# Chunk 2's second norm in a product buffer, and its turn one step later, in a one-core attention and GLU block

## The chip, the cores and the metric

The program runs on one core of a Trainium2 chip. The metric is the device time of one execution in microseconds (us); lower is better. Three timed runs of the kernel before have a median of 546.23 us (546.02 to 546.67). The profile is that of one execution, which has a time of its own.

A core has five engines that run side by side, each through its own list of instructions in order: TensorE (PE) multiplies matrices and turns tiles, VectorE (DVE) and ScalarE (ACT) work on elements, GpSimd (POOL) and SyncE (SP) mostly issue transfers (DMA). An instruction that waits holds up everything behind it in its engine's list. PE writes its results to PSUM, eight banks that other engines must empty ("evict") before they can be used again.

## The reference

```
x: 2048 rows of 576, bf16
mod = silu(c) @ w_mod                      -> sa, ca, ga, sb, cb, gb
h = layernorm(x) * (1 + ca) + sa           first norm
q, k, v = h @ wqkv                         32 heads of 18
attention of each row to 8 rows: itself and 2, 4, ... 14 rows back
x = x + ga * (attention @ wo)              called x1 in the kernel
h = layernorm(x) * (1 + cb) + sb           second norm
x = x + gb * (((h @ w_gate) * (h @ w_up)) @ w_down)     width 4608
```

`layernorm(v) = (v - mean) / sqrt(var + 1e-5)` over the 576 columns of a row.

## The kernel before

**Chunks and stages.** The rows are cut into 8 chunks of 256, each of 2 tiles of 128 rows. The GLU runs in five stages over groups of tiles: stage 0 takes chunk 0 (tiles 0 and 1), stage 1 chunks 1 and 2 (tiles 2 to 5), and so on. Each stage is a `gate_up` (36 blocks of 128 of the GLU's columns, `hh = gate * up`) and then a `down_pairs` (the sums with `w_down`; the last stage uses `down_last`). What the later chunks need (norms, queries, keys, values, attention, the product with `wo`) is laid between the matmuls of these stages as "pieces".

**The order is written by hand.** Nothing reorders it: each engine runs its instructions in the order in which the Python code issues them. In `down_pairs` the work of stage 0 is a list of 32 steps (8 blocks of `w_down`, 4 steps each; line 988), and the table `dbg` (line 1507) says which pieces are issued behind which step: an entry `(24, norm_x1_2)` is issued behind step 24, and an entry with a list such as `(27, b_parts(1))` puts its first half behind step 27 and its second behind step 28. Behind the 32 steps come the last sums of the stage over the last four blocks: with two tiles (line 1007) these are the narrow sums `run("r", 0, 1)`, the wide ones `run("a", 0, 1)`, then both with the row halves changed over, `gate_r()` and `gate(0)`, `gate(1)` on DVE, and the stores.

**Row halves.** Every matmul uses 64 of the 128 rows of the PE array, and two run side by side, so a step issues pairs: a wide one (`acc`, 512 columns) and a narrow one (`accr`, 64 columns).

**Turning a chunk.** A norm `xn` has rows on partitions and the GLU needs columns on partitions. `turn_unit` (line 611) does this on PE: `first()` takes two PSUM banks and turns 12 squares of 64 x 128, `second()` turns 8 more and then evicts six pieces with the modulation, three on DVE (line 332) and three on ACT (line 334). `b_parts(2)`, kept as `t2_2` (line 1506), is this for chunk 2's second norm; it writes `h2T`, which the first matmul of stage 1's `gate_up` reads. In `dbg` its first half stands behind step 30 and its second behind step 31. Other chunks are turned by DMA: `a_flip(4)`, behind step 29, issues two transposing DMAs from SP that read chunk 4's first norm and write `hT`. `a_mod(4)` then modulates `hT` in place early in stage 1, three parts on DVE and two on ACT, for the units of chunk 4's queries and keys, which begin behind block 3 of that `gate_up`.

**Chunk 2's second norm.** `norm_x1_2` (line 1486), behind step 24: ACT takes tile 0's mean and variance (lines 316 to 323), writing what it doesn't need into `junk`, a buffer of the pool `prodp`; DVE takes tile 1's (lines 1497, 1498) and ACT the square root (lines 1499, 1500); then DVE writes both normalized tiles into `xn` (line 1503), a buffer of the pool `lnp`.

**Pools.** A tile of a pool takes over the buffer of an older tile, and its first write waits until the last use of the older one has ended. `lnp` has 2 buffers. When `norm_x1_2` asks for one, chunk 1's second norm (read by `b_parts(1)`, steps 27 and 28) and chunk 4's first norm (read by `a_flip(4)`, step 29) are both still in use. `prodp` has 6, for the attention's products of queries and keys (line 481), which no chunk makes during the end of stage 0. The next products are those of chunk 3, early in stage 1.

Of the kernel before, what the change touches and what calls it, by code (L numbers as in the profile page):

```python
# [18 lines left out]
P = 128  # L19
# [30 lines left out]
def kernel(  # L50
# [253 lines left out]
        nc.scalar.activation(rstd, rstd, ACTF.Ln, bias=eps[:], scale=1.0 / D)  # L304
        nc.scalar.activation(rstd, rstd, ACTF.Exp, scale=-0.5)

    act_mv = []

    def act_norm(src, junk=None):
        xn = lnp.tile([P, ST, DP], BF, name="ln_xn") if junk is None else None  # L310
        junk = xn if junk is None else junk
        mv = small.tile([P, ST, 2], F32, name="ln_mva")
        act_mv.append(mv)

        def mean(j):
            nc.scalar.activation(junk[:, j, 0:D], src(j), ACTF.Identity, scale=-1.0 / D, accum_out=mv[:, j, 0:1])

        def square(j):
            nc.scalar.activation(junk[:, j, 0:D], src(j), ACTF.Square, bias=mv[:, j, 0:1], accum_out=mv[:, j, 1:2])

        def rsq(r=slice(0, ST)):
            nc.scalar.activation(mv[:, r, 1], mv[:, r, 1], ACTF.Ln, bias=eps[:], scale=1.0 / D)
            nc.scalar.activation(mv[:, r, 1], mv[:, r, 1], ACTF.Exp, scale=-0.5)

        def norm(j):
            for d0, s0, n in ((0, 0, D), (D, D - 64, 64)):
                nc.vector.tensor_scalar(xn[:, j, d0:d0 + n], src(j)[:, s0:s0 + n], mv[:, j, 0:1], mv[:, j, 1:2], ALU.add, ALU.mult)
        return xn, mean, square, rsq, norm
# [360 lines left out]
    def b_parts(i, cols=(0, 1)):  # L689
        def make():  # L690
            ht, o0 = h2_of(ST * i + cols[0])
            return turn_unit(bb[i]["xn"], cols, mod_evict(lambda m: ht[:, m, o0:o0 + P * len(cols)], cols, 2))
        return parts(make)
# [12 lines left out]
    def a_flip(i):  # L706
        return lambda: (a_tiles(i), flips(aa[i]["hT"], aa[i]["xn"]))
# [236 lines left out]
    def down_pairs(gi, hh, bg):  # L944
        for piece in bg.get(-1, ()):
            piece()
        t0, t1 = GROUPS[gi]
        nj = t1 - t0
        steps = down_steps(nj)
        acc = [ps([P, 512], F32, "acc") for _ in range(2)]  # L950
        accr = [ps([P, 2, 64], F32, "accr") for _ in range(3 if nj == 3 else 2)]
        acc += [ps([P, 512], F32, "acc") for _ in range(nj - 2)]
        o_ts, t_r = {}, {}
        seen, written, order, synced = set(), {}, [0], [-1]
        left = {("a", j): 2 * FT for j in range(nj)} | {("r", j): 2 * FT for j in range(nj)}

        def mm(kind, j, r, f):
            bank = (kind, j) if kind == "a" else (kind, j % len(accr))
            dst = acc[j][:] if kind == "a" else accr[j % len(accr)][:, j // len(accr), :]
            cs = slice(0, 512) if kind == "a" else slice(512, D)  # L960
            last_r, n, m = written.get(bank, (r, -1, None))
            if last_r != r and n > synced[0]:
                swap_after(m)
                synced[0] = n
            rows = (LO, HI)[r]
            left[kind, j] -= 1
            m = half(dst, hh[rows, f, js(j)], wd_blk[gi * NBLK + f // FB][rows, f % FB, cs], bank not in seen, left[kind, j] == 0)
            seen.add(bank)
            written[bank] = (r, order[0], m)
            order[0] += 1  # L970

        def pair(kind, lo, hi):
            for r, (j, f) in enumerate((lo, hi)):
                mm(kind, j, r, f)

        def gate(j):
            o_ts[j] = gup.tile([P, 512], BF, name="o_t", tag="g_sb" if j % 2 else "u_sb")
            nc.vector.tensor_tensor(o_ts[j][:], acc[j][:], gb_bc[:, 0:512], ALU.mult)

        def gate_r():  # L980
            t = smp.tile([P, nj, 64], BF, name="t_r", tag="tree")
            for k, a in enumerate(accr):
                n = len(range(k, nj, len(accr)))
                nc.vector.tensor_tensor(t[:, k:nj:len(accr), :], a[:, 0:n, :],
                                        gb_bc[:, None, 512:D].to_broadcast([P, n, 64]), ALU.mult)
            t_r[0] = t

        for n, (lo, hi, r_early, loaded) in enumerate(steps):
            fs = list(zip(lo, hi))
            for k, (a, b) in enumerate(fs):  # L990
                if r_early and k == len(fs) - 1:
                    pair("r", a, b)
                    pair("a", a, b)
                else:
                    pair("a", a, b)
                    pair("r", a, b)
            if loaded is not None and (gi > 0 or loaded not in (4, 5)):
                load_wd((5, 6, NBLK - 1, 7)[loaded] if gi == 0 and loaded < 4 else gi * NBLK + loaded + 3)
            for piece in bg.get(n, ()):
                piece()  # L1000
        f0 = FT - FB

        def run(kind, a, b):
            for f in range(f0, FT):
                pair(kind, (a, f), (b, f))

        if nj == 2:
            run("r", 0, 1)
            run("a", 0, 1)
            run("r", 1, 0)  # L1010
            gate_r()
            run("a", 1, 0)
            gate(0)
            gate(1)
        elif nj == 4:
            run("r", 0, 1)
            run("r", 2, 3)
            run("a", 0, 1)
            run("a", 2, 3)
            run("r", 1, 0)  # L1020
            run("r", 3, 2)
            gate_r()
            run("a", 1, 0)
            gate(0)
            gate(1)
            run("a", 3, 2)
            gate(2)
            gate(3)
        else:
            for k, (lo, hi) in enumerate(cycle_of_three(f0)):  # L1030
                for a, b in zip(lo, hi):
                    pair("a", a, b)
                    pair("r", a, b)
                if k == 4:
                    gate(1)
            gate_r()
            gate(0)
            gate(2)
        assert not any(left.values())
        for j in range(nj):  # L1040
            xt = x1[(t0 + j) // ST][(t0 + j) % ST]
            r0 = (t0 + j) * P
            nc.vector.tensor_tensor(xt[:, 0:512], o_ts[j][:], xt[:, 0:512], ALU.add)
            nc.vector.tensor_tensor(xt[:, 512:D], t_r[0][:, j, :], xt[:, 512:D], ALU.add)
            nc.sync.dma_start(out_flat[r0:r0 + P, :], xt[:])
        load_wd(gi * NBLK + NBLK + 2)
# [404 lines left out]
    w1, w2, w3, w4, w5, w6, w7 = [w_parts(i) for i in range(1, NCH)]  # L1451
    n3, n1, n4, n2 = {}, {}, {}, {}

    def begin(n, src):
        n.update(zip(("xn", "mean", "square", "rsq", "norm"), act_norm(src)))

    def stat_act(n, tiles=range(ST)):
        for j in tiles:
            n["mean"](j)
            n["square"](j)  # L1460
# [23 lines left out]
        n4["rsq"]()  # L1484

    def norm_x1_2():
        src = lambda j: x1[2][j]
        junk = prodp.tile([P, ST, DP], BF, name="prod")
        _, mean, square, rsq, _ = act_norm(lambda j: src(j)[:], junk)
        xn = bb[2]["xn"] = lnp.tile([P, ST, DP], BF, name="ln_xn")  # L1490
        mva = act_mv[-1]
        stats, mv = small.tile([P, ST, 2, 6], F32, name="ln_statsb"), small.tile([P, ST, 2], F32, name="ln_mvb")
        mean(0)
        square(0)
        rsq(slice(0, 1))
        for hf in range(2):
            nc.vector.bn_stats(stats[:, 1, hf, :], src(1)[:, hf * 288:(hf + 1) * 288])
        nc.vector.bn_aggr(mv[:, 1, :], stats[:, 1].rearrange("p a b -> p (a b)"))
        nc.scalar.activation(mv[:, 0, 0:1], mv[:, 1, 1:2], ACTF.Ln, bias=eps[:])
        nc.scalar.activation(mv[:, 0, 1:2], mv[:, 0, 0:1], ACTF.Exp, scale=-0.5)  # L1500
        for j, m, r, op in ((0, mva[:, 0, 0:1], mva[:, 0, 1:2], ALU.add), (1, mv[:, 1, 0:1], mv[:, 0, 1:2], ALU.subtract)):
            for d0, s0, n in ((0, 0, D), (D, D - 64, 64)):
                nc.vector.tensor_scalar(xn[:, j, d0:d0 + n], src(j)[:, s0:s0 + n], m, r, op, ALU.mult)

    q3, k3, qk4_3, v0_3, v1_3 = qkv_units(3, [(0, 0, 5)])[0]
    t2_2 = b_parts(2)
    dbg = {0: at((-1, [gb_row]), (-1, lambda: n3["rsq"]()), (0, o_parts(1)), (0, lambda: (norms(n3), load_x(5))), (2, lambda: av(4)),
                 (5, a_parts(3)), (6, stat4), (6, lambda: av(2)), (8, w1[0]), (10, w1[1]), (11, stat1), (12, q3), (13, lambda: av(3)), (14, k3), (15, lambda: av(14)),
                 (16, qk4_3), (18, v0_3[:1]), (18, lambda: norms(n1)), (19, o_parts(2)), (20, lambda: (norms(n4), load_x(6))), (21, v0_3[1:]), (22, w2[0]), (23, w2[1]),
                 (24, norm_x1_2), (25, v1_3), (27, b_parts(1)), (29, a_flip(4)), (FT - FB - 2, t2_2)),  # L1510
           1: at((0, w3[0]), (3, w3[1]), (4, o_flip(4)), (4, lambda: b_ln(3)), (7, lambda: b_norm(3)), (8, lambda: a_ln(6)), (9, b_flip(3)),
                 (11, w4[0]), (12, lambda: a_norm(6)), (14, w4[1]), (14, a_flip(6)), (15, lambda: b_ln(4)), (16, b_mod(3)),
                 (18, lambda: b_norm(4)), (20, b_flip(4)), (21, a_mod(6)), (27, b_mod(4))),
# [46 lines left out]
```

## Time and profile before

| | |
|---|---|
| median of three runs | 546.23 us (546.02 to 546.67) |
| the profiled execution: its own time | 545.34 us |
| its span, first to last instruction | 543.6 us |
| PE busy | 532.2 us, 98% of the span |
| DVE, ACT, POOL busy | 317.2, 258.9, 72.3 us |
| mean granted PE clock | 0.994 |
| DMA moved | 113.10 MB, 208 GB/s on average |

The same span in stretches, with the busy time of PE and the clock that it was granted:

| stretch, us | what runs | PE busy, us | granted clock |
|---|---|---|---|
| 0 to 46 | chunks 0 to 2 begin | 43.40 | 1.00 |
| 46 to 85 | most of stage 0's `gate_up` | 38.99 | 1.00 |
| 85 to 126 | its end, and stage 0's `down_pairs` | 36.01 | 0.92 |
| 126 to 192 | stage 1 | 66.00 | 1.00 |
| 192 to 450 | stage 1's end to stage 4's `gate_up` | 258.00 | 1.00 |
| 450 to 543 | the end | 89.85 | 1.00 |

A busy PE is not PE at its peak, since matmuls overlap and a busy time says nothing of the clock; so what is read is where PE is not busy, and where its clock is below 1. Times in the profile are us from the span's start. "L1503" is line 1503 of the kernel. A group line gives the engine, the line, the operation, what is written and what it is read from, how many, and in brackets the idle time before it and what ended it.

### The profile page before, as it was taken

The page shows a single profiled execution, that of the slowest core. Times are in us where ns is not written, and L with a number is a line of the kernel's source. Part 1 is how long each engine was busy: PE and PEld are TensorE (multiplying, and loading weights), DVE is VectorE, ACT ScalarE, POOL GpSimd, SP SyncE. Part 2 cuts the span into 40 slices and gives each one's busy share as a digit, 9 for nine tenths or more (in the row PEclk, how much of TensorE's full clock was granted, in tenths as well). Part 3 has the DMA queues.
Part 4 walks back from the last instruction along what each step waited for, and adds up shares of the span by engine and source line. Part 5 has one row for each costly group of instructions (what it writes and reads, how often), then busy time and mean ns, then how long its engine had stood idle before and what let it go on. Part 6 is the DMA issues. An engine that isn't in the chain of part 4 may idle for free.

```text
span 543.6 us, 17000 instructions
## 1 busy us (share of the span) xinstructions
PE 532.2 (98%) x7317; PEld 319.6 (59%) x7317; DVE 317.2 (58%) x775; ACT 258.9 (48%) x625; POOL 72.3 (13%) x117
## 2 busy tenths in 40 slices
PE   8999999969999999999999999999999999999997
PEld 4788887734644465555544445556666555565564
DVE  7887899948267855655367785635537624322203
ACT  2767687834656664111655552114566511556500
POOL 4301224111000101122000100111100013100010
PEclk9999999988999999999999999999999999999999
DMA  8999998997255997976635796854785766965021
GB/s 265 286 278 306 349 302 279 341 267 257 90 177 136 291 111 249 188 174 205 244 91 163 232 230 215 180 167 133 243 265 156 236 195 176 350 198 170 2 89 34
DMA packets 88406, 113.10 MB, mean 208 GB/s; under 512 B 21866, under 2 KB 76090, under 8 KB 88330
## 3 DMA queue, kind: packets, MB, share of 16 engines
q1 hardware_dynamic: 77072, 66.05, 44.9%
q0 software_dynamic: 11168, 45.81, 27.1%
q8 instruction: 57, 0.93, 0.7%
q14 instruction: 19, 0.16, 0.1%
q10 hardware_dynamic: 90, 0.15, 0.1%
HBM read 103.22 MB, written 4.48 MB: 198 GB/s over the span
## 4 chain that ended last, share of the span: by engine, by line
PE 92%; DVE 3%; DMA 2%; ACT 1%; SPq 1%; issue 1%; DVEq 0%; ACTq 0%
PE pg L568 29%; PE pu L568 23%; PE acc L568 18%; PE pp L568 9%; PE acc L1086 4%; PE accr L568 2%; PE lg L491 2%; DMA wqk<-in_A_wqkv_dram 1%; DVE prod L481 1%; DMA hT<-ln_xn 1%; PE pq L420 1%; PE pq L1213 1%; PE po L796 1%; PE pv L445 1%; PE accr L1090 1%
## 5 line engine op out<-in xcount | busy, mean ns | idle before, releaser
L568 PE MATMUL pg<-h2T,wgu 64*128 64x512 bf16 (+2 forms) x1440 | 279.8, 333 | 0.0
L568 PE MATMUL pu<-h2T,wgu 64*128 64x512 bf16 (+2 forms) x1440 | 278.7, 333 | 0.0
L568 PEld LDWEIGHTS <-wgu 64*128 64x128 bf16 x2880 | 140.6, 94 | 104.9 <-issue 0.2
L914 ACT CAST u_sb<-pu 128x512 bf16<-128x512 f32 (+2 forms) x180 | 90.3, 501 | 137.5 <-PE pg L568 136.7
L920 DVE TENSOR_TENSOR hh<-g_sb,u_sb 128x512 bf16<-128x512 bf16 (+2 forms) x180 | 66.3, 370 | 106.6 <-ACT g_sb L915 104.7
L568 PE MATMUL acc<-wd,hh 64*128 64x512 bf16 x888 | 115.8, 378 | 0.1
L568 PEld LDWEIGHTS <-hh 64*128 64x128 bf16 x1872 | 62.4, 95 | 51.9 <-issue 1.8
L915 ACT CAST g_sb<-pg 128x512 bf16<-128x512 f32 (+2 forms) x180 | 91.4, 508 | 0.0
L568 PE MATMUL accr<-wd,hh 64*128 64x64 bf16 x888 | 77.1, 189 | 0.0
L568 PE MATMUL pu<-h2T,wgr 64*128 64x512 bf16 (+2 forms) x180 | 60.1, 334 | 0.0
L568 PE MATMUL pg<-h2T,wgr 64*128 64x512 bf16 (+2 forms) x180 | 60.1, 334 | 0.0
L174 POOL DMA_DIRECT2D wd<-in_B_w_down_dram x38 | 28.8, 758 | 169.9 <-PE accr L568 80.9
L481 DVE TENSOR_TENSOR prod<-qT,kT 128x1280 bf16<-128x1280 bf16 x54 | 42.9, 823 | 4.3 <-ACT kT L398 4.3
L553 DVE TENSOR_TENSOR vsh<-vsh,attn 128x1152 bf16<-128x1152 bf16 x56 | 40.2, 752 | 3.8 <-DMA vsh<-vd 3.8
L666 DVE TENSOR_TENSOR x<-pp,ga_bc 128x288 bf16<-128x288 f32 x28 | 12.0, 453 | 30.2 <-PE pp L568 30.2
L568 PEld LDWEIGHTS <-wgr 64*128 64x128 bf16 x360 | 17.8, 94 | 14.4 <-issue 1.7
L568 PE MATMUL pp<-hT,wqk 64*128 64x256 bf16 x360 | 22.3, 269 | 0.0
L282 ACT ACTIVATE ln_rstdb<-ln_mvb,eps 128x2 f32<-128x2 f32 (+1 forms) x6 | 1.8, 295 | 42.8 <-DVE ln_mvb L279 42.8
L565 POOL COPY o_sb<-o_sb 128x64 bf16<-128x64 bf16 x10 | 3.1, 310 | 134.2 <-DVE o_sb L564 134.2
L560 DVE TENSOR_TENSOR vsh<-vsh 128x1152 bf16<-128x1152 bf16 x28 | 20.4, 751 | 0.0
L568 PE MATMUL pp<-wo,oT 64*128 64x288 bf16 x252 | 19.9, 283 | 0.0
L568 PEld LDWEIGHTS <-wqk 64*128 64x128 bf16 x360 | 17.2, 94 | 4.5
(274 smaller groups left out, 558.9 us busy)
## 6 DMA issues: line engine op xcount, KB each, us to landing
wgu<-in_B_w_gate_dram SPq DMA_DIRECT2D x45, 512.0 KB, 5.0
wgu<-in_B_w_up_dram SPq DMA_DIRECT2D x45, 512.0 KB, 5.7
wd<-in_B_w_down_dram POOLq DMA_DIRECT2D x38, 576.0 KB, 4.6
vsh<-vd POOLq DMA_DIRECT2D x14, 1152.0 KB, 8.7
x_r<-in_A_x_dram SPq DMA_DIRECT2D x8, 288.0 KB, 8.1
vsh<-in_B_w_down_dram POOLq DMA_DIRECT2D x4, 576.0 KB, 8.2
out_dram<-x SPq DMA_DIRECT2D x15, 144.0 KB, 7.0
x_t<-in_A_x_dram SPq DMA_DIRECT2D x7, 288.0 KB, 8.8
```

What stands on the lines that cost most here:

```text
L174: return nc.gpsimd.dma_start(wb[:], B_w_down[r0:r0 + FB * P, :].rearrange("(k p) n -> p k n", p=P))
L420: nc.tensor.matmul(pq[:, gi, :], lhsT=qk_w(kt, m), rhs=hT[:, kt, :], start=(kt == 0), stop=(kt == KT - 1))
L481: nc.vector.tensor_tensor(prod[:], aa[i]["qT"][:], aa[i]["kT"][:, :, off:off + CH], ALU.mult)
L491: nc.tensor.matmul(b["lg"][H * wl:H * (wl + 1), wq, :], lhsT=ind[:, m, :], rhs=b["prod"][4 * wq + wl][:, m, :], start=(m == 0), stop=(m == ...
L553: nc.vector.tensor_tensor(v, v, at, ALU.mult)
L560: nc.vector.tensor_tensor(vsh[:, d], vsh[:, d], vsh[:, 4 + 2 * s:6 + 2 * s], ALU.add)
L568: return nc.tensor.matmul(dst, lhsT=lhs, rhs=rhs, start=first, stop=last, skip_group_check=True)
L666: nc.vector.tensor_tensor(x1[i][j][:, cs], t[:, 0, :], ga_bc[:, cs], ALU.mult)
L914: nc.scalar.copy(u[:, 0:N], pu[:, 0:N])
L915: nc.scalar.copy(g[:, 0:N], pg[:, 0:N])
L920: nc.vector.tensor_tensor(hh[:, f, 0:N], g[:, 0:N], u[:, 0:N], ALU.mult)
L1086: nc.tensor.matmul(a[:], lhsT=hh[:, f, js(j)], rhs=wb[:, f % FB, cs], start=(f == 0), stop=(f == FT - 1))
```

## The change

The norm is computed as before; its result stays in the `prodp` buffer that was the `junk` before, so no `lnp` buffer is asked for. `act_norm` now takes the buffer from its caller. Tile 1's two writes keep their own line, tile 0's two are issued by `act_norm`'s `norm`. The entry of `t2_2` in `dbg` moves from step 30 to step 31, so its first half is issued behind the last step, and its second half behind "step 32", which doesn't exist as a step: `down_pairs` issues it in the last sums, between the second and the third of the four pairs of `run("a", 0, 1)`.

```diff
-    def act_norm(src, junk=None):
-        xn = lnp.tile([P, ST, DP], BF, name="ln_xn") if junk is None else None
-        junk = xn if junk is None else junk
+    def act_norm(src, xn):
         mv = small.tile([P, ST, 2], F32, name="ln_mva")
...
-        def run(kind, a, b):
-            for f in range(f0, FT):
+        def run(kind, a, b, fs=range(f0, FT)):
+            for f in fs:
                 pair(kind, (a, f), (b, f))
 
         if nj == 2:
             run("r", 0, 1)
-            run("a", 0, 1)
+            run("a", 0, 1, range(f0, f0 + 2))
+            for piece in bg.get(len(steps), ()):
+                piece()
+            run("a", 0, 1, range(f0 + 2, FT))
             run("r", 1, 0)
             gate_r()
             run("a", 1, 0)
...
+    def begin(n, src, room=None):
+        xn = room or lnp.tile([P, ST, DP], BF, name="ln_xn")
+        n.update(zip(("xn", "mean", "square", "rsq", "norm"), act_norm(src, xn)))
...
     def norm_x1_2():
-        src = lambda j: x1[2][j]
-        junk = prodp.tile([P, ST, DP], BF, name="prod")
-        _, mean, square, rsq, _ = act_norm(lambda j: src(j)[:], junk)
-        xn = bb[2]["xn"] = lnp.tile([P, ST, DP], BF, name="ln_xn")
-        mva = act_mv[-1]
+        begin(n2, lambda j: x1[2][j][:], prodp.tile([P, ST, DP], BF, name="prod"))
+        xn = bb[2]["xn"] = n2["xn"]
...
-        for j, m, r, op in ((0, mva[:, 0, 0:1], mva[:, 0, 1:2], ALU.add), (1, mv[:, 1, 0:1], mv[:, 0, 1:2], ALU.subtract)):
-            for d0, s0, n in ((0, 0, D), (D, D - 64, 64)):
-                nc.vector.tensor_scalar(xn[:, j, d0:d0 + n], src(j)[:, s0:s0 + n], m, r, op, ALU.mult)
+        n2["norm"](0)
+        for d0, s0, n in ((0, 0, D), (D, D - 64, 64)):
+            nc.vector.tensor_scalar(xn[:, 1, d0:d0 + n], x1[2][1][:, s0:s0 + n], mv[:, 1, 0:1], mv[:, 0, 1:2], ALU.subtract, ALU.mult)
...
-                 (24, norm_x1_2), (25, v1_3), (27, b_parts(1)), (29, a_flip(4)), (FT - FB - 2, t2_2)),
+                 (24, norm_x1_2), (25, v1_3), (27, b_parts(1)), (29, a_flip(4)), (FT - FB - 1, t2_2)),
```

FT is 36 and FB is 4, so `FT - FB - 2` is 30 and `FT - FB - 1` is 31.

More of the change, by code (lines that the diff above doesn't have):

```diff
@@ L305, in mean_var_on_act @@
         nc.scalar.activation(rstd, rstd, ACTF.Exp, scale=-0.5)
-    act_mv = []
-    def act_norm(src, junk=None):
-        xn = lnp.tile([P, ST, DP], BF, name="ln_xn") if junk is None else None
-        junk = xn if junk is None else junk
+    def act_norm(src, xn):
         mv = small.tile([P, ST, 2], F32, name="ln_mva")
-        act_mv.append(mv)
         def mean(j):
-            nc.scalar.activation(junk[:, j, 0:D], src(j), ACTF.Identity, scale=-1.0 / D, accum_out=mv[:, j, 0:1])
+            nc.scalar.activation(xn[:, j, 0:D], src(j), ACTF.Identity, scale=-1.0 / D, accum_out=mv[:, j, 0:1])
         def square(j):
-            nc.scalar.activation(junk[:, j, 0:D], src(j), ACTF.Square, bias=mv[:, j, 0:1], accum_out=mv[:, j, 1:2])
+            nc.scalar.activation(xn[:, j, 0:D], src(j), ACTF.Square, bias=mv[:, j, 0:1], accum_out=mv[:, j, 1:2])
         def rsq(r=slice(0, ST)):
@@ L1452 @@
     n3, n1, n4, n2 = {}, {}, {}, {}
-    def begin(n, src):
-        n.update(zip(("xn", "mean", "square", "rsq", "norm"), act_norm(src)))
+    def begin(n, src, room=None):
+        xn = room or lnp.tile([P, ST, DP], BF, name="ln_xn")
+        n.update(zip(("xn", "mean", "square", "rsq", "norm"), act_norm(src, xn)))
     def stat_act(n, tiles=range(ST)):
@@ L1486, in norm_x1_2 @@
     def norm_x1_2():
-        src = lambda j: x1[2][j]
-        junk = prodp.tile([P, ST, DP], BF, name="prod")
-        _, mean, square, rsq, _ = act_norm(lambda j: src(j)[:], junk)
-        xn = bb[2]["xn"] = lnp.tile([P, ST, DP], BF, name="ln_xn")
-        mva = act_mv[-1]
+        begin(n2, lambda j: x1[2][j][:], prodp.tile([P, ST, DP], BF, name="prod"))
+        xn = bb[2]["xn"] = n2["xn"]
         stats, mv = small.tile([P, ST, 2, 6], F32, name="ln_statsb"), small.tile([P, ST, 2], F32, name="ln_mvb")
-        mean(0)
-        square(0)
-        rsq(slice(0, 1))
+        stat_act(n2, (0,))
+        n2["rsq"](slice(0, 1))
         for hf in range(2):
-            nc.vector.bn_stats(stats[:, 1, hf, :], src(1)[:, hf * 288:(hf + 1) * 288])
+            nc.vector.bn_stats(stats[:, 1, hf, :], x1[2][1][:, hf * 288:(hf + 1) * 288])
         nc.vector.bn_aggr(mv[:, 1, :], stats[:, 1].rearrange("p a b -> p (a b)"))
```

## The prediction

> **What bounds the kernel now.** First I read who waits for whom, for PE alone over the whole span, since PE is busy in 98% of it:
>
> ```profile
> PE tr_pA L615 <- DVE ln_xn L1503: 4.6, 1, 4.6
> PE idle L209 <- DVE hT L204: 1.3, 1, 1.3
> PE pq L1213 <- DMA wqk<-in_A_wqkv_dram: 0.9, 2, 0.5
> ```
>
> The columns are total us, times and longest. PE has one long wait: the first half of chunk 2's turn waits 4.6 us for line 1503. The same view for all engines around it says what line 1503 waited for:
>
> ```profile
> DVE ln_xn L1503 <- DMA hT<-ln_xn: 5.8, 1, 5.8
> ```
>
> The chain that ended last, cut to this place (start, duration), confirms it:
>
> ```profile
> 114.88 5.16 DMA hT<-ln_xn
> 120.04 0.04 DVEq L1503
> ...
> 120.47 0.64 DVE ln_xn L1503 x2
> ```
>
> DVE's norm needs nothing from `hT`; it waits because its `lnp` buffer holds chunk 4's norm, which the transposing DMAs of step 29 still read until 120.04. Next the timeline of ACT and DVE (start, duration), to see when the operands were there:
>
> ```profile
> 114.14 0.21 DVE L1498 BATCH_NORM_AGGREGATE ln_mvb<-ln_statsb 128x2 f32<-128x12 f32 x1
> 120.13 0.64 DVE L1503 TENSOR_SCALAR ln_xn<-x,ln_mva 128x576 bf16<-128x576 bf16 x2 [5.78 <-DMA hT<-ln_xn]
> 120.68 0.63 DVE L1503 TENSOR_SCALAR ln_xn<-x,ln_mvb 128x576 bf16<-128x576 bf16 x2
> ...
> 114.53 0.20 ACT L323 ACTIVATE ln_mva<-ln_mva 128x1 f32<-128x1 f32 x1
> 114.95 0.20 ACT L1500 ACTIVATE ln_mvb<-ln_mvb 128x1 f32<-128x1 f32 x1
> 115.06 0.68 ACT L751 CAST v_sb<-pp 128x288 bf16<-128x288 f32 x2
> 115.63 1.39 ACT L334 ACTIVATE h2T<-tr_pB,modc 128x256 bf16<-128x256 bf16 x3
> ```
>
> Both tiles' statistics are complete at 114.73 and 115.15. Last, the busy time in stretches of 2 us (stretch, length, PE, PEld, DVE, ACT, POOL, granted clock, DMA):
>
> ```profile
> 114.00:116.00 2.00, 1.91 (x43) 0.82 (x34) 0.32 (x2) 1.90 (x9) 0.27 (x1) 1.00 1.53 165
> 116.00:118.00 2.00, 0.00 (x0) 0.00 (x0) 0.00 (x0) 1.01 (x3) 2.00 (x4) 1.00 1.29 98
> 118.00:120.00 2.00, 0.00 (x0) 0.00 (x0) 0.00 (x0) 0.00 (x0) 0.35 (x1) 0.61 0.59 202
> 120.00:122.00 2.00, 1.29 (x18) 0.73 (x20) 1.87 (x7) 0.00 (x0) 0.00 (x0) 0.50 1.05 369
> 122.00:124.00 2.00, 2.00 (x30) 0.97 (x26) 1.18 (x4) 1.19 (x3) 1.13 (x2) 0.50 0.54 184
> 124.00:126.00 2.00, 2.00 (x22) 0.98 (x20) 0.36 (x2) 0.18 (x1) 1.38 (x2) 0.68 0.81 212
> ```
>
> The stall costs twice. The clock is still 1.00 up to 118; 0.61 over the next 2 us puts its fall at 118.4, some 2.5 us into the wait. It stays at 0.50 until about 125.3 (0.68 over 124 to 126), 4.7 us after PE resumed at 120.61. Nowhere else in the front's stretches is it below 1.00.
>
> **The sum.** The stretch to price runs from the end of step 30's issue (last `accr` at 115.78, plus 0.03 = 115.81) to the first matmul of stage 1's `gate_up`, at 125.87: 10.06 us.
>
> What PE has to do in it, at full clock, from rows just before the stall: two wide and two narrow pairs of a step, 0.22 + 0.03 twice = 0.49 (114.15 to 114.64); the first half of a turn, 0.17, and the second, 0.12 (chunk 1's, 113.81 to 113.98 and 114.47 to 114.59); four narrow pairs, 4 x 0.03 = 0.12; four wide, half of 1.73 for eight in stage 1's last sums = 0.86. In the new order: step 31 0.49, first half 0.17, narrow 0.12, two wide 0.43, second half 0.12, two wide 0.43, narrow 0.12, wide 0.86. Sum 2.74.
>
> - *The removed wait.* DVE's first norm can start at 114.73 + 0.05 = 114.78. In the old trace the four writes take 120.13 to 121.31, 1.18 us, so they end at 115.96. The moved first half begins at 115.81 + 0.49 = 116.30: 0.3 us of slack. One step earlier it would have had to wait about 0.2, so the later place is worth that. Removed: 120.61 - 115.81 = 4.80.
> - *The slowed work.* From 120.61 to 125.87 PE took 5.26 for these 2.74. The difference, 2.52, is 4.67 us at half clock (2.33) and 0.2 of waiting for tile 1 inside the turn. It goes if PE no longer idles.
> - *A new wait.* The second half now ends later against `gate_up`. Its last turn ends at 116.30 + 0.17 + 0.12 + 0.43 + 0.12 + 0.16 = 117.30. ACT's three evictions took 1.37 (122.81 to 124.18), and ACT is through with chunk 1's at 117.02, so they end at 117.33 + 1.37 = 118.70. `gate_up` is due at 115.81 + 2.74 = 118.55 and reads the last of them first: with 0.05 for the signal it starts at 118.75. Cost 0.20. Before, 1.7 us of sums at half clock covered this. The bounds: nothing, if ACT's ends overlap; 0.8, if ACT starts half a us late.
> - *The buffers.* `xn` keeps its `prodp` buffer until 117.3; the next writer is line 481, behind `gate(1)` and four adds, which began 2.28 us after `gate_up` (128.15 against 125.87), hence at 121.0. That covers it: 0. Without that cover the product would wait under 1 us. `b_parts(1)`'s DVE evictions, queued behind line 1503, come at 116 instead of 121.2, so its two banks are free for `gate_up`'s first block.
> - *Where the wait goes.* DVE must still not modulate `hT` before 120.04. That is due 4.49 us after `gate_up` (130.36 against 125.87), at 123.2, and on ACT 4.18 after, at 122.9. Slack 2.9 us: 0.
> - *Queues.* SP issues nothing there but the transposes, before the stall. POOL's third `wd` load and the two `vsh` loads behind it (122.87, 123.61) waited for step 31 and move to about 118.4 and 119.1; the `vsh` loads read values written at 115.73 to 116.83, landing in 3.5 us, so POOL may wait until 120.3, with nothing behind it that is due. Weights for stage 1's first blocks were issued by 105.8, and 13 us is the median to landing, so the first block is there and the third lands around 118, due at 134. 0.
>
> Sum: -4.80 - 2.52 + 0.20 = -7.1 us. Every later stretch is PE at 100% and clock 1.00, and PE's list of waits names no other after 46 us, so the start of stage 1 carries through to the end. The profiled execution took 545.34 us (span 543.6 and 1.7 around it), so it would take 538.2. It lies 0.9 below the median of the runs; from that, **539.1**.
>
> The Trainium skill, "TensorE: Matmul & The Clock Gate", Part 1 (the HAM clock gate), says that full rate comes after some 3.4 us of sustained work. This trace shows 4.7 us from the resumption; by the page the half rate would cost 1.7 instead of 2.3, and the sum would be -6.5 and the time 539.7.
>
> **Rivals.**
> - *The wait is shortened, not gone* (chance 0.09). Some other releaser of line 1503 or of the turn comes at 117 to 118: for: ACT is busy without a gap from 112.49 to 117.02, so a single late ACT row shifts the turn and the evictions; against: each of them was in place by 117.02 in this trace. Up to 2 us comes back, below the 2.5 at which the clock fell: to 541.1. If it passes that, the 2.3 of clock comes back too: to 543.4.
> - *The transposes become slower* (0.03 for any loss, 0.02 more for slower than before). The `wd` and `vsh` loads now start beside them. The place is the modulation of `hT`: chunk 4's queries begin 7.07 us into `gate_up` (132.94), at 125.8, and PE waits there for landing + 0.85 us of DVE. The point from which it costs is a landing at 125.0; from 129.8 on (4.8 of stall, and the 2.3 of clock that a stall over 2.5 brings) the kernel is slower than before. If the transposes were starved until all later loads had drained (five loads, 4.1 MB at 369 GB/s from 118 on: 129.2) and then took 5.16, they land at 134.4, PE stalls 9.4 and the clock takes 2.3: 550.8. For: the DMA engines are nearly full from 120 on (1.05). Against: the first two `wd` loads were issued at 116.83 beside the transposes here, which still landed at 120.04, and the transposes go first.
> - The Trainium skill, "Trainium Kernel Development and Optimization", Key Constraints, says that the queues of all issuers share the same 16 DMA engines and interleave, which is what that rival needs; the 1.29 and 0.59 at 116 to 120 show the sharing without harm.
> - *The change doesn't do what it says* (0.03): the `prodp` buffer has a late reader too. Then 546.2. Against: ACT already wrote its junk there at 112.49, waiting only for DVE's line 668; in the built program line 1503's successor waits for ACT alone, and the wait for the two DMAs stands at the modulation of `hT`.
>
> **How the numbers follow.** The forecast has 0.83, the others 0.09, 0.05, 0.03. Its own spread is the run-to-run one (546.02 to 546.67, and 545.34 profiled: 0.9 down) and the new wait's 0 to 0.8. Range: at the bottom 538.0, the profiled time less 7.3 (no new wait); at the top 541.1, where the first rival's milder half is held and some 0.1 is left above. A change below 0.2% (1.1 us) can't be told from none. Faster by more: forecast, first rival and the mild part of the second, 0.94; within: 0.04, the third rival and a rest; slower: 0.02.
>
> **What would show it.** In the profile after: no row for line 1503's successor waiting on a DMA; its first write near 114.8; PE's wait for the turn gone from the list; clock 1.00 in all stretches from 114 to 130; `gate_up` of stage 1 starting near 118.7; at most some 0.2 us of PE idle before it, put down to ACT; `hT`'s modulation near 123 with no wait for the DMA. The prediction is wrong if PE idles over 1 us between 115 and 126, if the clock falls there, or if the 7 us are lost again behind 126.

## The result and the profile after

The changed kernel takes 538.59 us (median of four runs, 538.06 to 539.64) against 546.12 for the kernel before in the same comparison: a ratio of 0.9864, 95% interval 0.9846 to 0.9883. That is 7.5 us less, with an interval of 6.4 to 8.4. The profiled execution took 538.30 us (span 536.6) against 545.34 (543.6): 7.0 less.

The changed kernel's lines after the edit at `act_norm` are numbered 5 lower, and those of the planning functions 2 to 5 lower: its line 563 is the old 568, its line 327 the old 332. Line 1503 became two: 322 (tile 0, issued by `act_norm`) and 1498 (tile 1).

First the list of PE's waits, over the whole span (total us, times, longest):

```profile
PE idle L209 <- DVE hT L204: 1.3, 1, 1.3
PE pg L563 <- issue: 1.1, 1, 1.1
PE pq L1211 <- DVE vsh L327: 0.5, 1, 0.5
```

The wait for the norm is gone. The second line is new, but it is not of the change: it stands at 80.85 us, 31 us ahead of the first instruction that the change touches, and PE reaches the end of step 30 only 0.05 us later than in the trace before. Four of the experiments below have such a wait at this place, of 0.4 to 1.1 us, two of them without the change of buffer, and the others have none.

Then DVE and ACT around the turn, by the timeline (start, duration, and in brackets the idle time before and what ended it):

```profile
114.19 0.21 DVE L1493 BATCH_NORM_AGGREGATE ln_mvb<-ln_statsb 128x2 f32<-128x12 f32 x1
114.81 0.64 DVE L322 TENSOR_SCALAR prod<-x,ln_mva 128x576 bf16<-128x576 bf16 x2 [0.41 <-ACT ln_mva L318]
115.36 0.64 DVE L1498 TENSOR_SCALAR prod<-x,ln_mvb 128x576 bf16<-128x576 bf16 x2
115.91 0.98 DVE L327 TENSOR_SCALAR h2T<-tr_pA,modc 128x256 bf16<-128x256 bf16 x3
...
123.22 0.85 DVE L327 TENSOR_SCALAR hT<-hT,modc 128x256 bf16<-128x256 bf16 x3
...
117.39 1.37 ACT L329 ACTIVATE h2T<-tr_pB,modc 128x256 bf16<-128x256 bf16 x3 [0.33 <-PE tr_pA L610]
```

The norm starts at 114.81 instead of 120.13, released by ACT. The modulation of `hT`, which now carries the wait for the transposing DMAs, starts at 123.22 with no idle time in front: the DMAs were in time for it.

PE's own timeline at the turn and at the start of stage 1:

```profile
116.35 0.19 PE L610 MATMUL tr_pA<-ident,prod 64*128 64x64 bf16 x1
...
117.85 1.04 PE L563 MATMUL acc<-wgu,hh 64*128 64x512 bf16 x8
118.81 0.37 PE L563 MATMUL pg<-h2T,wgr 64*128 64x512 bf16 x1
```

The turn has no bracket: PE does not idle in front of it. `gate_up` starts at 118.81 instead of 125.87. And the stretches of 2 us, in the columns of before:

```profile
116.00:118.00 2.00, 2.00 (x56) 1.23 (x52) 1.46 (x5) 1.67 (x5) 2.00 (x4) 1.00 1.36 106
118.00:120.00 2.00, 2.00 (x20) 0.96 (x18) 1.74 (x6) 0.76 (x2) 1.14 (x2) 1.00 0.84 302
120.00:122.00 2.00, 2.00 (x22) 1.03 (x19) 2.00 (x7) 0.00 (x0) 1.60 (x2) 1.00 0.99 332
122.00:124.00 2.00, 2.00 (x22) 1.03 (x19) 2.00 (x6) 1.97 (x5) 0.17 (x1) 1.00 1.03 353
```

PE is busy throughout and its clock stays at 1.00. From the start of step 30's last narrow pair to `gate_up`, the stretch that the prediction summed, it is 118.81 - 115.83 = 2.98 us; before it was 125.87 - 115.78 = 10.09. The difference is 7.1 us, and the spans differ by 7.0: what was gained there stayed gained.

### The profile page after: what moved, and what is told of

It reads as the page before. It is cut to its first block, busy times and chain, and to the rows that moved or that the text cites. A ratio compares the mean times of both kernels' runs of the same rounds, so it can differ in the third digit from the quotient of the medians.

```text
span 536.6 us, 17000 instructions
## 1 busy us (share of the span) xinstructions
PE 529.0 (99%) x7317; PEld 320.3 (60%) x7317; DVE 317.6 (59%) x775; ACT 259.1 (48%) x625; POOL 72.9 (14%) x117
## 4 chain that ended last, share of the span: by engine, by line
PE 94%; DVE 2%; DMA 1%; issue 1%; SPq 1%; ACT 1%
PE pg L563 29%; PE pu L563 23%; PE acc L563 19%; PE pp L563 9%; PE acc L1084 4%; PE accr L563 3%; PE lg L486 2%; DMA wqk<-in_A_wqkv_dram 1%; DVE prod L476 1%; PE pq L415 1%; PE po L791 1%; PE pq L1211 1%; PE pv L440 1%; PE accr L1088 1%; PE pwj L805 0%
```

## The experiments

All eight use the stretch from step 30's last narrow pair to the first matmul of stage 1's `gate_up`. The changed kernel and the two in which one norm alone is moved agree in it to 0.03 us, while medians of a few runs are good to some 1 us. The stretch is that of the one profiled execution, and where the clock falls it differs between executions of one kernel. Ratios are against the kernel before, in the same comparison. In these comparisons the kernel before took 546.12 us (changed kernel), 545.85 (buffer alone, move alone, chunk 4's norm, 27 pairs), 544.99 (20 pairs) and 546.22 (the other three), so kernels are compared by the ratios and not by the medians.

| kernel | stretch, us | clock in it | median, us | ratio (95% interval) |
|---|---|---|---|---|
| before | 10.09 | falls to 0.50 | 546.12 | 1 |
| changed | 2.98 | 1.00 | 538.59 | 0.9864 (0.9846 to 0.9883) |
| buffer alone | 2.95 | 1.00 | 539.09 | 0.9884 (0.9867 to 0.9900) |
| move alone | 9.89 | falls to 0.50 | 545.48 | 0.9998 (0.9971 to 1.0026) |
| chunk 4's norm moved instead | 2.95 | 1.00 | 538.97 | 0.9894 (0.9860 to 0.9927) |
| stall filled, 27 pairs | 8.24 | 1.00 | 543.70 | 0.9965 (0.9955 to 0.9976) |
| stall filled, 20 pairs | 9.82 | falls to 0.50 | 543.54 | 0.9972 (0.9954 to 0.9990) |
| stall filled, 15 pairs | 10.25 | falls to 0.50 | 544.41 | 0.9965 (0.9942 to 0.9987) |
| second half later | 3.52 | 1.00 | 539.41 | 0.9857 (0.9816 to 0.9897) |
| both halves at step 31 | 3.14 | 1.00 | 538.77 | 0.9876 (0.9797 to 0.9956) |

**The buffer alone.** The changed kernel with the turn back at its old place.

```diff
-                 ... (FT - FB - 1, t2_2)),
+                 ... (FT - FB - 2, t2_2)),
```

> Chunk 2's norm in the product buffer, its turn at the old place (first half behind step 30, second behind step 31). Theory (the wait for the lnp buffer is the whole cost, the later place is worth 0.2 us at most): DVE's first write starts near 114.8, PE waits 0.1 to 0.4 us inside the turn for tile 1, the clock stays at 1.00, gate_up of stage 1 starts within 0.3 us of the changed kernel's 118.8, time 538.2 to 539.0. Rival (the later place brings a good part of the gain): PE stalls over 1 us at the old place, time 540 to 544.

Measured: 2.95 us, and no wait for DVE in PE's list. This trace is 0.5 us behind that of the changed kernel all along, and its times are shifted by that:

```profile
115.34 0.64 DVE L322 TENSOR_SCALAR prod<-x,ln_mva 128x576 bf16<-128x576 bf16 x2 [0.41 <-ACT ln_mva L318]
115.89 0.64 DVE L1498 TENSOR_SCALAR prod<-x,ln_mvb 128x576 bf16<-128x576 bf16 x2
```

The norm ends at 116.53, and step 30 at 116.39. The turn reads tile 0 first, so it starts at once, and only its last two squares come 0.05 us late, where 0.1 to 0.4 us of waiting were expected. The buffer alone brings the whole gain; the rival falls.

**The move alone.** The kernel before with the turn one step later and its second half in the last sums.

```diff
-            run("a", 0, 1)
+            run("a", 0, 1, range(f0, f0 + 2))
+            for piece in bg.get(len(steps), ()):
+                piece()
+            run("a", 0, 1, range(f0 + 2, FT))
...
-                 ... (FT - FB - 2, t2_2)),
+                 ... (FT - FB - 1, t2_2)),
```

> Chunk 2's norm in the lnp buffer as before, its turn one step later with the second half in the last sums. Theory: line 1503 still waits for the two transposing DMAs until about 120.0; PE's stall begins one step later and is 0.5 us shorter (some 4.1 us), the clock falls all the same, gate_up starts near 125.2, time 545.2 to 545.9. Rival (the place is what matters): 539 to 543.

Measured: a ratio of 0.9998, no difference. The waits of PE, from the same list:

```profile
PE tr_pA L615 <- DVE ln_xn L1506: 4.3, 2, 4.0
```

The stall is 0.6 us shorter, 0.49 for the step in front of it and 0.16 because PE is that much later in this trace, but the stretch is only 0.2 shorter. The rest is lost behind the stall. The turn's first half waits longer for tile 1: from its start to the next matmul it takes 1.15 us, against 0.81 before. And the clock rose again at 126.3, in the execution before at 125.3, so all of the sums ran at half rate. The expected 0.7 us were too many.

**Another buffer.** The kernel before, except that chunk 4's first norm lies in a product buffer; chunk 2's stays in `lnp`.

```diff
-        begin(n4, lambda j: x[:, j, :])
+        begin(n4, lambda j: x[:, j, :], prodp.tile([P, ST, DP], BF, name="prod"))
```

> As before, but chunk 4's first norm (which the transposing DMAs read) lies in a product buffer, and chunk 2's norm stays in lnp; turn at the old place. Theory (the wait was for the one buffer that chunk 4's norm holds): the wait is gone as in the kernel with the buffer alone, first write near 114.8, clock 1.00, time 538.2 to 539.0. Rival (something else of DVE's or PE's order holds the norm or the turn until the DMAs land): line 1503 still starts near 120, time 545 to 546.5.

Measured: 2.95 us, as with the buffer alone. The norm's first write, by the timeline (this trace is 0.5 us ahead of that of before):

```profile
114.26 0.64 DVE L1503 TENSOR_SCALAR ln_xn<-x,ln_mva 128x576 bf16<-128x576 bf16 x2 [0.41 <-ACT ln_mva L323]
```

The transposing DMAs are the same as ever, and line 1503 again writes to `lnp`; it no longer waits for them, since they no longer read what lay in its buffer. So the wait was for the buffer and not for anything in the order of the engines.

**The stall filled.** The kernel before with dummy matmuls in pairs behind step 30, into columns of the `accr` banks that nothing reads. They shorten no wait; they keep PE busy in it.

```diff
-        accr = [ps([P, 2, 64], F32, "accr") for _ in range(3 if nj == 3 else 2)]
+        accr = [ps([P, 8, 64], F32, "accr") for _ in range(3 if nj == 3 else 2)]
...
+                    m = half(accr[k][:, 2:8, :].rearrange("p a b -> p (a b)"), ident[rows, :], wgr[rows, 0:384], False, False)
...
+            if gi == 0 and n == FT - FB - 2:
+                keep_busy(27)
```

> As before, with 27 pairs of dummy matmuls of 384 columns behind step 30, some 4.4 us of PE work in the stall, into columns of the accr banks that nothing reads. Theory (half the loss behind the stall is the clock): line 1503 starts near 120.1 as before, the clock stays at 1.00, from the end of the turn's first half at 121.4 the rest takes 2.6 instead of 4.45 us, gate_up starts near 124.0, time 544.0 to 544.5. Rival (the stall alone costs, the low clock is only shown): 545.8 to 546.5.

Measured: the stretch is 1.85 us shorter, 8.24 against 10.09, and the median 2.2 below that of before in this comparison (543.70 against 545.85; 544.0 to 544.5 was expected). PE's timeline, and two stretches of 2 us behind it:

```profile
115.26 4.55 PE L568 MATMUL accr<-wgr,ident 64*128 64x384 bf16 x54
119.98 0.20 PE L615 MATMUL tr_pA<-ident,ln_xn 64*128 64x64 bf16 x1 [0.17 <-DVE ln_xn L1514]
...
123.47 0.38 PE L568 MATMUL pg<-h2T,wgr 64*128 64x512 bf16 x1
```

```profile
118.00:120.00 2.00, 1.83 (x26) 0.90 (x22) 0.50 (x2) 0.00 (x0) 0.00 (x0) 1.00 0.96 345
120.00:122.00 2.00, 1.87 (x42) 1.09 (x44) 1.95 (x8) 0.41 (x1) 0.26 (x1) 1.00 0.97 334
```

The norm comes about as late as before: the turn starts 4.75 us after step 30's last pair, against 4.83. From the turn's start to `gate_up` it is 3.49 us against 5.26, and these 1.8 us are the clock; all nine executions have a mean granted clock of 0.999 or 1.000. So of the 7.1 us some 1.8 were work at half rate, and the rest the stall and the waits inside the turn.

**The stall filled by half** (15 pairs in place of 27).

> As before, with 15 pairs of dummy matmuls of 384 columns behind step 30, some 2.45 us, into columns of the accr banks that nothing reads, so that 2.2 us of idle time are left in front of the turn. Theory (the clock falls some 2.5 us into an idle time): it stays at 1.00, gate_up starts near 124.0, time 544.0 to 544.5. Rival (a shorter idle time is enough): the clock falls within the 2.2 us or right after, time 545.5 to 546.5.

Measured: the theory falls, though the median of 544.41 lies in its range, as that of a mix of executions with and without a low clock. PE idled 2.58 us, and the clock did not fall in it but after PE had resumed:

```profile
122.13 0.20 PE L615 MATMUL tr_pA<-ident,ln_xn 64*128 64x64 bf16 x1 [2.58 <-DVE ln_xn L1514]
```

```profile
120.00:122.00 2.00, 0.00 (x0) 0.00 (x0) 0.36 (x2) 0.00 (x0) 0.00 (x0) 1.00 0.87 311
122.00:124.00 2.00, 1.74 (x38) 1.14 (x40) 1.72 (x8) 0.05 (x1) 0.00 (x0) 0.83 1.06 364
124.00:126.00 2.00, 2.00 (x24) 0.91 (x20) 0.97 (x3) 1.32 (x3) 1.99 (x3) 0.50 0.66 118
126.00:128.00 2.00, 2.00 (x19) 0.75 (x18) 0.98 (x4) 0.00 (x0) 0.52 (x1) 0.82 0.85 332
```

In stretches of 0.2 us the fall is at 123.3 and the rise at 126.7, 3.4 us apart. In the kernel before they are at 118.46 and 125.28, and with the move alone at 119.50 and 126.33: both 6.8 apart, twice 3.4. The clock also falls behind PE's last matmul, at the end of this trace:

```profile
541.00:543.00 2.00, 0.15 (x2) 0.00 (x0) 1.03 (x4) 0.00 (x0) 0.00 (x0) 1.00 0.39 123
543.00:544.90 1.90, 0.00 (x0) 0.00 (x0) 0.00 (x0) 0.00 (x0) 0.00 (x0) 0.54 0.13 39
```

In stretches of 0.02 us this fall is at 543.15, 416.43 us after the rise at 126.73; with the move alone the last fall is at 542.76, also 416.43 us after the rise. That is 122 times 3.413. So this is no timer that starts with the idle time, but a judgement at the ends of fixed windows. The Trainium skill ("TensorE: Matmul & The Clock Gate", Part 1, "What's actually happening") says so: a free-running window of 3413 ns. The traces agree, with 3.4, 6.8 and 6.8. Where the windows lie differs from execution to execution: of the ten here, three have a mean clock of 1.000 (542.97 to 543.48 us), one 0.998 (544.34), three 0.997 (544.20 to 544.98) and three 0.995 (544.75 to 546.65). The fall at the end counts in this mean too, by 0.0016 here: the profiled execution's 0.995 is one window in the stretch and the end, and a 0.998 can be the end alone. So the clock fell at the stall in six or seven of the ten.

**The stall mostly filled** (20 pairs), to see how little idle time is enough.

> As before, with 20 pairs of dummy matmuls behind step 30, some 3.4 us, into columns of the accr banks that nothing reads, so that 1.2 to 1.8 us of idle time are left in front of the turn. Theory (the clock is decided at the end of fixed windows of some 3.4 us, by the share of the window that PE was idle; 65% was enough, in the run with 2.6 us of idle time, and now it is at most 50%): the granted clock is 0.999 or 1.000 in every execution, time 543.4 to 544.0. Rival (half a window of idle time is enough too): some executions at 0.995 to 0.997 as with 15 pairs, median 544.2 or more.

Measured: three of ten executions at 0.997 (544.52, 545.24, 545.46 us), the other seven at 0.999 or 1.000 (542.87 to 544.28). The theory's time holds (543.4 to 544.0 expected, median 543.54), but its claim on the clock falls: 1.34 us of idle time can be enough. The profiled execution is one of the three:

```profile
120.01 0.20 PE L615 MATMUL tr_pA<-ident,ln_xn 64*128 64x64 bf16 x1 [1.34 <-DVE ln_xn L1514]
```

```profile
118.00:120.00 2.00, 0.67 (x10) 0.20 (x4) 0.48 (x2) 0.00 (x0) 0.00 (x0) 1.00 0.92 329
120.00:122.00 2.00, 1.86 (x38) 1.17 (x40) 1.62 (x7) 0.06 (x1) 0.01 (x1) 0.77 1.02 353
122.00:124.00 2.00, 2.00 (x24) 0.90 (x20) 0.95 (x3) 1.31 (x3) 2.00 (x3) 0.50 0.57 118
```

The clock fell at 121.1, with 1.34 us of idle time and 0.8 us of the turn's twelve squares in the 3.4 us in front of it. With 27 pairs the same 0.8 us of turn and 0.17 idle never brought it down. The Trainium skill ("TensorE: Matmul & The Clock Gate", Part 4, PE-mode transpose) says that transposes do not count as PE work in the same way; with them left out, 2.1 of the 3.4 us were empty here. These runs fit that but do not isolate it, for there is a second reading: twelve squares take 0.17 us when the norm is there, so 0.63 of the 0.8 us were waiting for its pieces, and 1.97 us were empty even if the squares count.

The ends of the traces narrow down the share that is needed, with other matmuls in front of it. With 15 pairs the window that closes at 543.15 holds 2.00 us without a matmul, and the clock falls. In the traces of the kernel before and of 20 pairs, windows counted on from the rise close 1.86 and 1.90 us behind PE's last matmul, and the clock stays. By this, 1.34 us of idle time alone would not have been enough, so the turn did not count as full work. An estimate from these numbers: to hold nearly all of the 2.14 us from 118.67 to 120.81, a window of 3.4 us has some 1.3 us of places, four in ten; three in ten were seen.

**The second half later.** The changed kernel with the turn's second half behind all of `run("a", 0, 1)` and `run("r", 1, 0)`.

> The changed kernel with the second half of the turn behind the wide pairs and the turned-over narrow pairs, 0.55 us later. Theory (what is left in front of gate_up is the wait for ACT's last eviction): the wait grows from 0.2 to some 0.7 us, gate_up starts near 119.35, time 0.5 us above the changed kernel's 538.6. Rival (the evictions are hidden): gate_up stays near 118.8.

Measured, by the timeline:

```profile
118.74 0.37 PE L563 MATMUL pg<-h2T,wgr 64*128 64x512 bf16 x1 [0.58 <-ACT h2T L329]
```

The wait for ACT's last eviction shows itself, with 0.58 us, and the stretch grows by 0.54. So this wait is what limits how late the second half may be, and the changed kernel, whose wait is 0.09, stands just at its edge. The median can't tell 0.5 us.

**Both halves behind step 31.** The changed kernel with `t2_2`'s halves one right after the other.

> The changed kernel with both halves of the turn behind step 31, the second 0.55 us earlier. Theory: ACT's evictions end near 118.2, before PE is there, so the wait before gate_up goes, but PE waits some 0.15 us between the halves for the row tiles to change banks: gate_up starts at 118.6 to 118.9, time within 0.3 us of the changed kernel's 538.6. Rival (splitting the halves is worth more): a wait of 0.5 us or more for DVE or ACT inside the turn, time 539.2 or more.

Measured: 3.14 us, 0.16 more than the changed kernel and 0.07 above the top of what was expected: PE's second half starts 0.26 us after the last start of the first, where 0.03 is the pace within a half, and the wait before `gate_up` is gone. One of its four executions took 545.04 us at a mean clock of 0.995, and one of six of the kernel with chunk 4's norm moved took 542.89 at 0.996; neither was profiled, and what stopped PE in them is open.

## Why the prediction was right

The time, 539.1 forecast and 538.59 measured, came out of the terms in the way that they were summed.

- *The wait removed.* The norm was to start at 114.78 and did at 114.81; the turn at 116.30, and did at 116.35 (PE was 0.05 late when it got there). That the wait was for the buffer is shown twice, by moving chunk 2's norm out and by moving chunk 4's.
- *The slowed work.* 2.52 us were put on it, 2.33 of them the clock. The filled stall gives some 1.8 for the clock alone. The sum for the stretch was the same, because what is left, the turn's waits for tile 1, goes with the late norm and not with the clock. The step was right for its purpose, but the split was 0.5 us off.
- *What brings the clock down* was read wrongly: the fall "2.5 us into the wait" was taken for a limit of idle time, and the first rival's price rested on it. The runs with 2.58 and 1.34 us of idle time show that it can fall after PE has resumed, with as little as 1.34 us in front of a turn that itself waits. By the windows, the 4.7 us from PE's start to the rise are the 1.26 us left of one window and all of the next, 3.41. Nothing in the forecast itself hung on it, since no idle time was left.
- *The later place* was put at 0.2 us and is worth nothing that can be seen: 2.95 us at the old place and 2.98 at the new one. The old place was given the whole 0.2 between the norm's end and the turn's start, but the first half reads tile 0 first.
- *The new wait* before `gate_up` was put at 0.20. PE's last wide pairs start at 117.85 and four take 0.87, so it was due at 118.72 and started at 118.81: 0.09.
- *The buffers* were put at nothing, and line 481's first write, due at 121.0, started at 121.01 behind its adds without waiting.
- *Where the wait went.* `hT`'s modulation was due at 123.2 on DVE and 122.9 on ACT, and started at 123.22 and 122.99 without waiting. POOL's third `wd` load and the `vsh` loads moved as said, the latter to 120.40, behind an idle time of 1.3 us, and their earlier start did not hold the transposes up: the transposes landed 5.1 us after issue (median) against 5.5 before.
- *The rest of the span* was to carry the gain through, and did, with 7.0 us of 7.1. The rival in which the transposes become slower was not tried by itself; the changed kernel's trace shows them in time by 3 us.

## What to carry to other kernels

A wait can be for a buffer and not for data: here the norm's operands were ready 5.4 us before it ran, and the releaser that the profile named, a DMA that reads another chunk's tile, had no part in its computation. Then look for a buffer that is already held and idle (here the one for the statistics' throwaway output), and check when its next user comes.

Price a stall of PE with the clock behind it, since a stall of 4.6 us cost 7.1, some 1.8 of it by the clock; and do not count on a short gap being free, since here 1.3 us of idle time in front of a turn that itself waited for its tiles went with a lower clock in three of ten executions.

When two edits come together, try each alone: here one brought everything and the other nothing that can be measured.

## What was not expected of the hardware

The mean granted clock of the kernel before is not one number. Over 45 executions in three comparisons, 32 have 0.989 to 0.994 (median 545.8 us) and 13 have 0.995 or 0.997 (median 544.9); one more took 3166.38 us, at a clock of 1.000, and is left out. A span of 544 us with one low window of 3.4 us has a mean of 0.997, and with two, 0.994. The end of the program, where PE has nothing left to do, took up to 0.0016 more in the traces: in the changed kernel's profiled execution, with 0.998, the clock falls only at 534.95 of 536.6 us. So the position of the windows, which no kernel here sets, would make part of the spread from run to run. This is argued and not tested: within the comparisons the two groups' medians lie 1.1, 0.7 (with two executions in one group) and 0.15 us apart. The low clock does go with the stall: of 22 executions of the five kernels without it, 20 have 0.998 or more.
